# Rows of q dealt to chosen DMA engines: one batch or three

## The chip, the core and the metric

The kernel runs on one core of a Trainium2 chip. The metric is device time in microseconds (us), the median of several runs. A core has five engines with their own instruction streams: PE (matrix products and transposes), DVE and ACT (elementwise work, PSUM to SBUF copies, activations), POOL (here little but the issue of loads) and SP (the issue of the first load and of the outputs). Sixteen DMA engines move data between HBM and SBUF for all of them. A transfer that POOL issues is laid out over DMA engines row by row, each engine works through its own queue in order, and a transfer has landed when all sixteen engines have given their completion mark.

## The reference

Inputs are q, k and v, each (8 batches, 8 heads, 576 rows, 64), the weights `moe_w_r` and `moe_w_i`, each (64 modes, 512, 512), and `moe_w_ch` (512, 512), all float32. Cut to what matters:

```python
scores = scale * np.matmul(q, k.transpose(0, 1, 3, 2))
mask = (rel >= 0) & (rel < 64)                 # causal, a window of 64
attn = softmax(np.where(mask, scores, -1e9))
x = matmul(attn, v) -> (batch, 576, 512)       # heads side by side

X = np.fft.rfft(x, axis=1)                     # along the 576 rows
Yr = Xr @ w_r[m] - Xi @ w_i[m]                 # for each of the first 64 modes m
Yi = Xr @ w_i[m] + Xi @ w_r[m]
y = np.fft.irfft(Y, n=S, axis=1)
u = x + y
return u + np.maximum(u @ w_ch, 0.0)
```

127 weight matrices of 1 MB are read once (mode 0 has no imaginary part), besides 28 MB of q, k, v. The output is 9.4 MB.

## The kernel before

**Attention (0 to about 142 us).** For each batch, `load` brings q, k and v as raw rows in bf16 (the DMA casts): tile `rq` holds `[128, 2, 18 * 64]`. Partition p of half x holds 18 consecutive sequence rows of one head: four heads make the lower half, four the upper one. `transpose_units` gives twelve units for a batch; `part` turns six of the 18 rows' blocks at a time on PE against an identity matrix (`ident_bf`) and copies the result to `qT`, `kT` or `vT`, `vback` turns v once more. `scores`, `weigh` and `mask` make windows of scores, exponentials on ACT and the weighted sums; `dft` and `dft_turn` make the 64 modes of x into `XQ`. PE's and POOL's orders are written out by hand in this part; DVE's and ACT's are the scheduler's. A unit that has read a raw tile calls `refill`, which issues the load of the same tensor two batches on (two buffers each), and with it one weight.

**Modes (about 142 to 392 us).** `half(i)` takes weight i through sixteen products of 128 x 16 against `XQ`; `issue` refills the ring of weight buffers as they are read. In between, PE works on the product with `w_ch` and on the inverse transform. **Tail.** `final` adds, rectifies and stores through SP.

All loads but the first k are issued by POOL, in the order of the program. Eight completion semaphores are used in turn, so a transfer's issue waits for the landing of the transfer eight before it. In a transfer of 128 rows, each DMA engine takes eight rows.

**One q is dealt out unevenly.** `UNEVEN` is batch 7's q. Its lower half is issued as 125 rows for five DMA engines (25 each), the upper half as a plain transfer of 128 rows, then the three rows left over and a small transfer of 22 rows of 16 elements into `aside`. The view `"(r a) c -> a r c"` puts five outermost, and row r * 5 + a goes to partition a * 25 + r, so the rows stand in another order on the partitions. `part` undoes that: for the lower half of this q it uses `back` in place of `ident_bf`, a matrix that DVE makes from `ident_bf` with two copies (L262, L263). Transfers over fewer than sixteen engines begin, as the code has it, where the one before ended, in turn; the small transfer over eleven engines brings the turn round to its beginning.

In issue order the POOL transfers are counted from 0; the q of batches 5, 6 and 7 are 24, 30 and 36 (to 39).

Of the kernel before, what the change touches and what calls it, by code (L numbers as in the profile page):

```python
# [11 lines left out]
BF16 = mybir.dt.bfloat16  # L12
# [8 lines left out]
def view(ap, off, dims):  # L21

    return bass.AP(ap.tensor, ap.offset + off, [list(ap.ap[0])] + [list(d) for d in dims])
# [3 lines left out]
def kernel(  # L27
# [10 lines left out]
    nc = tc.nc  # L38
    B, H, S, D = q.shape
# [8 lines left out]
    RUN = S // 32  # L48
# [6 lines left out]
    def evac(o, i, on_act):  # L55

        if on_act:
            return nc.scalar.copy(out=o, in_=i)  # L58
        return nc.vector.tensor_copy(out=o, in_=i)  # L59
# [10 lines left out]
    ident_bf = consts.tile([128, 128], BF16, name="ident_bf")  # L70
# [19 lines left out]
    acons = p1.enter_context(tc.tile_pool(name="acons", bufs=1, side="right"))  # L90
# [12 lines left out]
    def raw_tile(which):  # L103
        return rawp.tile([128, 2, RUN * D], BF16, name="r" + which)

    def runs(b, which):
        return RAW[which][b].rearrange("(x g) (p c) d -> (g p) x (c d)", g=4, c=RUN)

    UNEVEN = (B - 1, "q")
    FEW, MORE = 5, 25
    LOT = FEW * MORE
    aside = acons.tile([2 * (16 - FEW), 16], BF16, name="aside")
    back = acons.tile([128, 128], BF16, name="back")

    def load(b, which):
        r = raw_tile(which)
        if (b, which) == UNEVEN:
            lower, upper = [RAW[which][b, x * H // 2:(x + 1) * H // 2].rearrange("g (p c) d -> (g p) (c d)", c=RUN)  # L120
                            for x in range(2)]
            nc.gpsimd.dma_start(out=r[:LOT, 0, :], in_=lower[:LOT].rearrange("(r a) c -> a r c", a=FEW))
            nc.gpsimd.dma_start(out=r[:, 1, :], in_=upper)
            nc.gpsimd.dma_start(out=r[LOT:, 0, :], in_=lower[LOT:])
            nc.gpsimd.dma_start(out=aside, in_=lower[:2 * (16 - FEW), 0:16].rearrange("(r a) c -> a r c", a=16 - FEW))
        else:
            nc.gpsimd.dma_start(out=r, in_=runs(b, which))
        raws[b, which] = r
# [65 lines left out]
    with tc.manual_schedule(engines=ALL_FOUR):  # L194
# [3 lines left out]
        with tc.tile_pool(name="tmpf", bufs=1, side="right") as tmp:  # L198
            mo = tmp.tile([128, NM], FP32, name="mo")
            to = tmp.tile([128, NT], FP32, name="to")  # L200
            nc.gpsimd.iota(mo, pattern=[[1, NM]], base=0, channel_multiplier=0,
                           allow_small_or_imprecise_dtypes=True)
            nc.gpsimd.iota(to, pattern=[[128, NT]], base=0, channel_multiplier=1,
                           allow_small_or_imprecise_dtypes=True)
            nc.gpsimd.memset(ident, 0.0)
            nc.gpsimd.affine_select(out=ident, in_=ident, compare_op=ALU.not_equal, fill=1.0,
                                    base=0, pattern=[[-1, 128]], channel_multiplier=1)
            load(0, "q")
            load(0, "v")
            for t0, t1 in ((0, 3), (3, NT)):  # L210
                n = t1 - t0
                mt = tmp.tile([128, 2, n * NM], FP32, name="mtf")
                nc.vector.tensor_tensor(out=view(mt, 0, [[NM, n], [1, NM]]), in0=view(mo, 0, [[0, n], [1, NM]]),
                                        in1=view(to, t0, [[1, n], [0, NM]]), op=ALU.mult)
                gen_trig(tmp, mt, n * NM, trigF[:, t0:t1, 0:NM], trigF[:, t0:t1, NM:2 * NM], "f")
                if t0 == 0:
                    nc.vector.tensor_copy(out=ident_bf, in_=ident)
        nc.scalar.activation(out=spark, in_=ident[:, 0:1], func=ACT_F.Exp)
        raws[0, "k"] = raw_tile("k")
        for c, engine in enumerate((nc.vector, nc.gpsimd, nc.vector)):  # L220
            cc = slice(6 * D * c, 6 * D * (c + 1))
            engine.tensor_copy(out=raws[0, "k"][:, :, cc], in_=k_first[:, :, cc])
        load(1, "k")
        for i in range(4):
            half = i % 2
# [24 lines left out]
    def transpose_units(b):  # L250

        rk, rq, rv = (raws.pop((b, which)) for which in "kqv")
        qT = qtp.tile([128, 4, S], BF16, name="qT")
        vT = vtp.tile([128, 4, S], BF16, name="vT")
        kT, vt = kTs[b % 2], vts[b % 2]
        qTs[b] = qT

        def part(src, dst, c0, on_act, uneven=False):
            def f():
                ps = ps_misc.tile([128, 6, 128], BF16, name="pst", tag="misc")  # L260
                if uneven and c0 == 0:
                    nc.vector.tensor_copy(out=back, in_=ident_bf)  # L262
                    nc.vector.tensor_copy(out=view(back, 0, [[1, FEW], [FEW, MORE]]),  # L263
                                          in_=view(ident_bf, 0, [[MORE, FEW], [1, MORE]]))
                for c in range(6):
                    for hh in range(2):
                        nc.tensor.transpose(out=ps[64 * hh:64 * hh + 64, c, :],  # L267
                                            in_=src[:, hh, (c0 + c) * D:(c0 + c + 1) * D],
                                            identity=back if uneven and hh == 0 else ident_bf)
                evac(view(dst, c0, [[S, 4], [RUN, 32], [1, 6]]),  # L270
                     view(ps, 0, [[32, 4], [1, 32], [128, 6]]), on_act)
            return f

        def vback(u):
            def f():
                ps = ps_misc.tile([128, 6, 128], BF16, name="psv", tag="misc")
                for i in range(6):
                    a, j = divmod(6 * u + i, 9)
                    if j == 4:
                        parts = [(0, 64, 2 * a, 512), (64, 64, 2 * a + 1, 0)]  # L280
                    else:
                        parts = [(0, 128, 2 * a + (j > 4), 128 * j - (j > 4) * S)]
                    for r0, n, g, t0 in parts:
                        nc.tensor.transpose(out=ps[r0:r0 + n, i, :],  # L284
                                            in_=vT[:, g, t0:t0 + n], identity=ident_bf)
                evac(view(vt, 6 * u * VW, [[18 * VW, 2], [VW, 6], [1, D]]),
                     view(ps, 0, [[D, 2], [128, 6], [1, D]]), u != 1)
                if u:
                    hs = slice(u - 1, u + 2, 2)
                    nc.vector.tensor_copy(out=vt[64:128, 1, hs, 1:9], in_=vt[64:128, 0, hs, 0:8])  # L290
                    nc.vector.tensor_copy(out=vt[0:64, 1, hs], in_=vt[0:64, 0, hs])
            return f

        return [part(rk, kT, 0, True), part(rk, kT, 6, False), part(rk, kT, 12, True),
                part(rv, vT, 0, False), part(rv, vT, 6, True), part(rv, vT, 12, False),
                *(part(rq, qT, 6 * i, i != 1, (b, "q") == UNEVEN) for i in range(3)),
                vback(0), vback(1), vback(2)]

    def head_of(n):
# [48 lines left out]
    def closes(w):  # L348

        return min(-(-8 * w // 9) * 9 or 9, 8 * w + 8)  # L350
# [92 lines left out]
    with tc.manual_schedule(engines=ALL_FOUR):  # L443
        first = transpose_units(0)
        for j in (0, 1, 2, 6, 7, 8):
            first[j]()
            refill(0, j)
            if j in (2, 8):
                warm_up(3)
        for half in range(2):  # L450
            pp = slice(64 * half, 64 * half + 64)
            nc.vector.tensor_copy(out=band2[pp], in_=band[pp, half, :])
        mask(0, 1)
        scores(0)
        for j in (3, 4, 5):
            first[j]()
            refill(0, j)
            warm_up(2)
        for vt in vts:
            nc.vector.memset(vt[:, 0, :, :, 64:66], 1.0)  # L460
        for j in (9, 10, 11):
            first[j]()
            refill(0, j)
        nc.vector.memset(pso, 1.0)
        nc.vector.tensor_copy(out=ident_r, in_=ident)
    with tc.manual_schedule(engines={E.PE, E.Pool}):
# [9 lines left out]
        def unit(b, j):  # L476
            if b not in units:
                units[b] = transpose_units(b)
            units[b][j]()
            refill(b, j)  # L480
            turned(b, j)

        for w in range(NWIN + 1):
# [5 lines left out]
            n = len(todo)  # L489
            if 0 < w < NWIN:  # L490
                scores(w)
            if w:
                cut = closes(w - 1)
# [12 lines left out]
            if w in (NWIN - 4, NWIN - 1):  # L506
                i = (B - 2) % 2 if w == NWIN - 4 else (B - 1) % 2
                spare(kTs[i])
                spare(qtp.tile([128, 4, S], BF16, name="qT"))
            if w in (NWIN - 4, NWIN):  # L510
                i = (B - 2) % 2 if w == NWIN - 4 else (B - 1) % 2
# [386 lines left out]
    for k, (f, delta, n, few) in enumerate(items):  # L898
        i = S_I + k * (T_I - 2 - S_I) // len(items)
# [25 lines left out]
    with tc.manual_schedule(engines=ALL_FOUR):  # L925
# [92 lines left out]
        for k in range(6):  # L1018
# [10 lines left out]
                              in_=view(psys[0], 0, [[2 * B, NC], [2, B], [1, 2]]))  # L1029
# [78 lines left out]
```

## Time and profile before

| | us |
|---|---|
| median of 3 runs | 424.34 (424.32 to 424.75) |
| the profiled execution | 424.43 |
| its span, first to last instruction | 422.7 |
| last weight issued, landed | 375.12, 389.20 |
| from there to the end of the span | 33.5 |
| PE busy | 352.8 (83%) |
| DVE, ACT, POOL busy | 189.0, 159.9, 83.7 |
| software DMA queue, packets' time as a share of 16 engines' span | 96.3% |

How to read it: DMA shares add up the time that packets were under way, and packets of one engine overlap a little, so a full engine shows a share over 1. In views by stretches the columns are the busy time of each engine with the number of instructions, then the granted clock of PE, the DMA share and the GB/s written. In a timeline a row is start, length, engine, line, operation, out<-in, and in brackets the idle time before it and what ended it. "DMA to landing" is the time from the issue to the last of the sixteen completion marks. L numbers are lines of the kernel before.

### The profile page before, as it was taken

The page shows a single profiled execution, that of the slowest core. Times are in us where ns is not written, and L with a number is a line of the kernel's source. Part 1 is how long each engine was busy: PE and PEld are TensorE (multiplying, and loading weights), DVE is VectorE, ACT ScalarE, POOL GpSimd, SP SyncE. Part 2 cuts the span into 40 slices and gives each one's busy share as a digit, 9 for nine tenths or more (in the row PEclk, how much of TensorE's full clock was granted, in tenths as well). Part 3 has the DMA queues.
Part 4 walks back from the last instruction along what each step waited for, and adds up shares of the span by engine and source line. Part 5 has one row for each costly group of instructions (what it writes and reads, how often), then busy time and mean ns, then how long its engine had stood idle before and what let it go on. Part 6 is the DMA issues. An engine that isn't in the chain of part 4 may idle for free.

```text
span 422.7 us, 11472 instructions
## 1 busy us (share of the span) xinstructions
PE 352.8 (83%) x5185; PEld 232.3 (55%) x5185; DVE 189.0 (45%) x361; ACT 159.9 (38%) x267; POOL 83.7 (20%) x149
## 2 busy tenths in 40 slices
PE   7899999999998779955758586757699998998994
PEld 3565666656654566744546455545466565554441
DVE  6576766775764100634342251211114344340895
ACT  5566866766765100122102110200023343330863
POOL 6231322232222230412112011210121212300000
PEclk9999999999999655978666656777569999999998
DMA  8999999999999999999999999999999999996598
GB/s 209 212 213 212 214 214 212 212 213 209 214 214 213 214 214 262 213 215 214 215 214 215 213 215 213 216 213 215 213 215 213 215 213 214 213 215 131 205 371 319
DMA packets 30288, 92.55 MB, mean 219 GB/s; under 512 B 2720, under 2 KB 2720, under 8 KB 30240
## 3 DMA queue, kind: packets, MB, share of 16 engines
q0 software_dynamic: 24992, 81.21, 96.3%
q1 hardware_dynamic: 5248, 10.62, 6.8%
q8 instruction: 40, 0.66, 0.6%
q14 instruction: 8, 0.07, 0.0%
HBM read 162.53 MB, written 9.44 MB: 407 GB/s over the span
## 4 chain that ended last, share of the span: by engine, by line
DMA 45%; PE 39%; DVE 7%; issue 2%; ACT 2%; DVEq 0%; POOLq 0%; ACTq 0%
DMA wms<-in_moe_w_i_dram 23%; DMA wms<-in_moe_w_r_dram 22%; PE psy L638 6%; PE pso L363 6%; PE pst L267 5%; PE psv L284 3%; PE psx L385 3%; PE pss L983 3%; DVE x_sb L371 2%; PE pss L976 2%; PE pss L320 2%; PE pss L339 2%; PE psz L779 2%; DVE vT L59 2%; PE psy L923 2%
## 5 line engine op out<-in xcount | busy, mean ns | idle before, releaser
L779 PE MATMUL psz<-wch,xT 128*128 128x512 f32 x144 | 61.2, 564 | 0.0
L773 DVE CAST xT<-pxt 128x1024 fp32r<-128x1024 bf16 x18 | 22.0, 1224 | 80.7 <-PE pxt L768 80.7
L782 ACT CAST Z<-psz 128x1024 fp32r<-128x1024 f32 x18 | 18.2, 1012 | 100.5 <-PE psz L779 100.5
L345 ACT ACTIVATE et<-pss 128x512 bf16<-128x512 f32 x72 | 39.2, 599 | 13.7 <-PE pss L339 13.7
L638 PE MATMUL psy<-XQ,wms 128*128 128x16 bf16 x624 | 25.0, 192 | 20.1 <-DMA wms<-in_moe_w_i_dram 12.3
L638 PE MATMUL psy<-XQ,wls 128*128 128x16 bf16 x560 | 21.9, 192 | 23.2 <-DMA wls<-in_moe_w_r_dram 14.4
L638 PEld LDWEIGHTS <-wms 128*128 128x128 bf16 x624 | 21.3, 102 | 32.3 <-DMA wms<-in_moe_w_i_dram 15.5
L779 PEld LDWEIGHTS psz<-wch,xT 128*128 128x128 f32 x144 | 34.9, 268 | 5.4
L638 PEld LDWEIGHTS <-wls 128*128 128x128 bf16 x560 | 19.6, 105 | 32.6 <-DMA wls<-in_moe_w_r_dram 17.2
L363 PE MATMUL pso<-vt,et 128*64 128x65 bf16 (+1 forms) x576 | 32.3, 203 | 3.5 <-DVE x_sb L371 1.6
L831 DVE TENSOR_TENSOR Z<-pse,Z 128x1024 fp32r<-128x1024 f32 x16 | 19.6, 1225 | 29.6 <-PE pse L820 29.6
L363 PEld LDWEIGHTS <-et 128*64 128x64 bf16 (+1 forms) x576 | 22.2, 108 | 14.2 <-issue 6.7
L371 DVE TENSOR_TENSOR x_sb<-pso,rcp 128x640 bf16<-128x640 f32 x32 | 26.3, 823 | 0.9
L638 PEld LDWEIGHTS <-wt 128*128 128x128 bf16 x560 | 18.4, 105 | 11.1 <-issue 4.2
L638 PE MATMUL psy<-XQ,wt 128*128 128x16 bf16 x560 | 20.5, 192 | 4.4 <-DMA wt<-in_moe_w_i_dram 1.7
L59 DVE COPY vT<-pst 128x768 bf16<-128x768 bf16 x16 | 15.3, 958 | 12.9 <-PE pst L267 11.3
L1001 ACT ACTIVATE pss<-pss 128x512 f32<-128x512 f32 x35 | 18.5, 581 | 4.7 <-PE pss L983 4.0
L59 DVE CAST YT<-psy 128x256 fp32r<-128x256 f32 x6 | 2.5, 423 | 38.6 <-PE psy L638 38.6
L923 PE MATMUL psy<-trigF,ident_bf 128*128 128x512 bf16 x46 | 18.4, 465 | 0.1
L284 PE MATMUL psv<-ident_bf,vT 128*128 128x128 bf16 (+1 forms) x160 | 15.7, 226 | 0.8 <-DVE vT L59 0.6
L320 PE MATMUL pss<-band,ident_bf 64*64 64x512 bf16 x120 | 16.3, 396 | 0.0
L58 ACT COPY vt<-psv 128x768 bf16<-128x768 bf16 x16 | 12.9, 808 | 8.5 <-PE psv L284 8.4
(198 smaller groups left out, 615.0 us busy)
## 6 DMA issues: line engine op xcount, KB each, us to landing
wt<-in_moe_w_i_dram POOLq DMA_DIRECT2D x19, 512.0 KB, 17.9
wt<-in_moe_w_r_dram POOLq DMA_DIRECT2D x16, 512.0 KB, 17.1
wls<-in_moe_w_r_dram POOLq DMA_DIRECT2D x8, 1024.0 KB, 21.7
wms<-in_moe_w_i_dram POOLq DMA_DIRECT2D x7, 1024.0 KB, 22.0
wms<-in_moe_w_r_dram POOLq DMA_DIRECT2D x7, 1024.0 KB, 21.2
wls<-in_moe_w_i_dram POOLq DMA_DIRECT2D x6, 1024.0 KB, 20.7
rv<-in_v_dram POOLq DMA_DIRECT2D x8, 576.0 KB, 13.0
rq<-in_q_dram POOLq DMA_DIRECT2D x7, 576.0 KB, 14.9
```

The costliest lines, as they stand in the source:

```text
L59: return nc.vector.tensor_copy(out=o, in_=i)
L267: nc.tensor.transpose(out=ps[64 * hh:64 * hh + 64, c, :], in_=src[:, hh, (c0 + c) * D:(c0 + c + 1) * D], identity=back if uneven and hh == ...
L284: nc.tensor.transpose(out=ps[r0:r0 + n, i, :], in_=vT[:, g, t0:t0 + n], identity=ident_bf)
L320: nc.tensor.matmul(out=pss[(2 * w + hh) % 3][64 * half:64 * half + 64, :], lhsT=ident_bf[pp, pp], rhs=view(band[pp], 128 * half, [[0, WIN ...
L345: nc.scalar.activation(out=et[:, hh, :], in_=pss[(2 * w + hh) % 3], func=ACT_F.Exp, scale=EX_SCALE)
L363: nc.tensor.matmul(out=pso[po, hh, block(b, i // 2) * VW:block(b, i // 2) * VW + D + 1], lhsT=et[pk, hh, col:col + 64], rhs=vt[pk, 1 - f % ...
L371: nc.vector.tensor_tensor(out=view(x_sb, b * NT * DM + g * D, [[4 * D, 2], [DM, NT], [1, D]]), in0=view(pso, 0, [[512, 2], [VW, NT], [1, D]]),
L638: nc.tensor.matmul(out=view(psy, off + 2 * B * e, [[1, 2 * B]]), lhsT=w[:, c, 128 * e:128 * e + 128], rhs=XQ[:, m // HM, c, :, 1 - im:3 - ...
L773: nc.vector.tensor_copy(out=o, in_=i)
L779: nc.tensor.matmul(out=psz[s][:, j, :], lhsT=xts[s % 2][0][:, j, 128 * c:128 * c + 128], rhs=wch[:, c, :], start=(c == 0), stop=(c == NC - 1))
L831: nc.vector.tensor_tensor(out=z, in0=ps, in1=z, op=ALU.add)
L923: nc.tensor.matmul(out=o, lhsT=ident_bf, rhs=view(trigF, 0, [[1, DM]]), start=True, stop=True)
```

## The change

Three q are dealt out unevenly in place of one. For each, `UNEVEN` gives the engines n, the rows m for each, the columns c (of 18) that are dealt, and the engines that a small transfer behind steps the turn on:

- batch 5: five engines, 25 rows each; a step of two
- batch 6: two engines, 28 rows each; a step of four
- batch 7: 34 rows in one lot for one engine (written as 17 x 2, which no number up to 16 divides), 16 of the 18 columns; a step of two

The rows left over (3, 72 and 94) follow the upper half in a transfer of their own; for batch 7 the last two columns of all 128 lower rows are a transfer too (128 pieces of 128 elements). The small transfers read k. 5 + 2 + 2 + 4 + 1 + 2 is 16. The three q take thirteen transfers in place of six (4, 4 and 5, where it was 1, 1 and 4). `back` is now one matrix for each of the three forms, and `part` uses it for the lower half of the dealt columns. PE has the same instructions in the same order but for the identity matrix; DVE has four copies more, at the start, right behind the two that it had; POOL has seven transfers more.

```diff
-    UNEVEN = (B - 1, "q")
-    FEW, MORE = 5, 25
-    LOT = FEW * MORE
-    aside = acons.tile([2 * (16 - FEW), 16], BF16, name="aside")
-    back = acons.tile([128, 128], BF16, name="back")
+    UNEVEN = {(5, "q"): (5, 25, RUN, 2), (6, "q"): (2, 28, RUN, 4), (7, "q"): (17, 2, 16, 2)}
+    for lot in UNEVEN.values():
+        assert lot[0] <= 16 or all(lot[0] % d for d in range(2, 17))
+    assert sum((n if n <= 16 else 1) + x for n, m, c, x in UNEVEN.values()) % 16 == 0
+    aside = [acons.tile([34, 16], BF16, name=f"aside{i}") for i in range(len(UNEVEN))]
+    forms = {lot[:2]: acons.tile([128, 128], BF16, name=f"back{lot[0]}") for lot in UNEVEN.values()}
+    made = set()
+
+    def back(key):
+
+        n, m = form = UNEVEN[key][:2]
+        if form not in made:
+            made.add(form)
+            nc.vector.tensor_copy(out=forms[form], in_=ident_bf)
+            nc.vector.tensor_copy(out=view(forms[form], 0, [[1, n], [n, m]]),
+                                  in_=view(ident_bf, 0, [[m, n], [1, m]]))
+        return forms[form]
+
+    def step_on(key, n):
+
+        n, src = (n if n > 1 else 17), k[0, :H // 2].rearrange("g (p c) d -> (g p) (c d)", c=RUN)
+        nc.gpsimd.dma_start(out=aside[list(UNEVEN).index(key)][:2 * n],
+                            in_=src[:2 * n, 0:16].rearrange("(r a) c -> a r c", a=n))
 
     def load(b, which):
         r = raw_tile(which)
-        if (b, which) == UNEVEN:
+        if (b, which) in UNEVEN:
...
-            nc.gpsimd.dma_start(out=r[:LOT, 0, :], in_=lower[:LOT].rearrange("(r a) c -> a r c", a=FEW))
+            n, m, c, behind = UNEVEN[b, which]
+            cut = lower[:n * m].rearrange("(r a) c -> a r c", a=n)
+            nc.gpsimd.dma_start(out=r[:n * m, 0, :c * D], in_=cut[:, :, :c * D])
             nc.gpsimd.dma_start(out=r[:, 1, :], in_=upper)
-            nc.gpsimd.dma_start(out=r[LOT:, 0, :], in_=lower[LOT:])
-            nc.gpsimd.dma_start(out=aside, in_=lower[:2 * (16 - FEW), 0:16].rearrange("(r a) c -> a r c", a=16 - FEW))
+            if c < RUN:
+                nc.gpsimd.dma_start(out=r[:, 0, c * D:], in_=lower[:, c * D:])
+            nc.gpsimd.dma_start(out=r[n * m:, 0, :c * D], in_=lower[n * m:, :c * D])
+            if behind:
+                step_on((b, which), behind)
...
-                                            identity=back if uneven and hh == 0 else ident_bf)
+                                            identity=back((b, which)) if hh == 0 and c0 + c < turned else ident_bf)
```

## The prediction

> **What bounds the kernel now.** I read the page's slices first, then its queues and chain, then the end of the chain, and last what POOL issues around the q of batch 7.
>
> ```profile
> DMA  8999999999999999999999999999999999996598
> GB/s 209 212 213 212 214 214 212 212 213 209 214 214 213 214 214 262 213 215 214 215 214 215 213 215 213 216 213 215 213 215 213 215 213 214 213 215 131 205 371 319
> ...
> q0 software_dynamic: 24992, 81.21, 96.3%
> ...
> q8 instruction: 40, 0.66, 0.6%
> ```
>
> The DMA engines are full and at one rate (213 GB/s written) from the first slice to the 36th; in the attention part and in the tail:
>
> ```profile
> 74.00:110.00 36.00, 35.08 (x753) 23.38 (x749) 24.65 (x46) 25.84 (x46) 10.08 (x17) 1.00 1.09 212
> 110.00:142.00 32.00, 27.71 (x487) 15.88 (x483) 16.80 (x34) 17.22 (x33) 6.36 (x12) 0.97 1.06 214
> ...
> 389.20:422.70 33.50, 27.41 (x137) 13.47 (x137) 24.46 (x40) 19.65 (x37) 0.00 (x0) 0.96 0.76 282
> ```
>
> (Busy PE, weight loads, DVE, ACT, POOL in us, then granted clock, DMA share, GB/s.) The 40 packets of q8 fetch instructions, 16 KB each. The end of the chain of waits:
>
> ```profile
> 374.20 0.90 issue
> 375.10 0.02 POOLq L1103
> 375.12 14.08 DMA wms<-in_moe_w_i_dram
> 389.20 0.05 issue
> 389.25 0.65 PE psy L638 x16
> ```
>
> The last weight is issued 14 us before it lands, and lies behind other rows all that time. What follows it (422.7 - 389.2 = 33.5 us) hangs on its landing alone. So the time is the slowest DMA engine's stream plus a fixed tail, and a change counts by what it does to that engine.
>
> The trace holds sixteen completion marks for each transfer, one an engine. Those of the last transfer, in us against the last of them:
>
> ```
> -6.25 -5.94 -5.36 | -1.90 -1.75 -1.34 -1.21 -0.91 -0.75 -0.57 -0.56 -0.55 -0.48 -0.44 -0.29 0
> ```
>
> Three engines end 5.4 to 6.3 us early; thirteen lie within 1.9 us. The mean is 1.77 us ahead of the last, so a perfect division at no cost would bring 1.77 us. The reason shows in the marks too: after each q8 fetch one engine's marks jump back by 1.0 to 1.4 us and recover part; the fetches' lengths repeat with period eight (893, 893, 949, 944, 936 to 940, 975, 975, 962 ns), so eight engines seem to fetch and eight not. The five that took the 125 rows of batch 7 were among the early ones before and the five last ones right after (0 to 0.65 us behind, the next 2.3 us ahead of them). The three left over are the early three.
>
> **What the old form cost** is seen at the issues on POOL:
>
> ```profile
> 88.97 0.70 POOL L122 DMA_DIRECT2D rq<-in_q_dram  x1 [2.24 <-PE pst L267]
> 89.68 0.57 POOL L123 DMA_DIRECT2D rq<-in_q_dram  x1
> 91.42 0.73 POOL L124 DMA_DIRECT2D rq<-in_q_dram  x1 [1.17 <-DMA rq<-in_q_dram]
> 93.89 0.56 POOL L125 DMA_DIRECT2D aside<-in_q_dram  x1 [1.73 <-DMA wt<-in_moe_w_r_dram]
> ```
>
> In the packet records a 2304-byte row (one q row) starts every 173 ns on an engine, a 4096-byte one every 305. A line through both gives 154 ns for a 2048-byte row and 22 ns for a 256-byte piece (estimates from these rows). The eleven engines outside the five each show 25 four-byte packets 6 ns apart for the 125-row transfer: padding, 0.155 us with its completion. The 3-row transfer and the aside cost an engine outside them some 0.033 us each. Over 35 to 43 (transfers by issue order) the front engine needed 11.42 us where rows and completions alone make 11.20: the padding is paid.
>
> **The change, part by part.** I number engines from the turn's start: 0 to 4 the five lots, then 5, 6 skipped, 7 and 8 the two, 9 to 12 skipped, 13 the one, 14 and 15 skipped. The trace does not number them.
>
> *Rows.* Lower halves of q5, q6, q7. An engine of 0-6 or 9-12 gave 16 even rows (2.77 us) for two of these batches, and the 25-row lot is the same before and after. Now it gives 5 of the 72 rows, 6 of the 94 short rows and 8 pieces: 0.865 + 0.924 + 0.176 = 1.965. That is -0.80 us for eleven engines. 7 and 8: -0.80 + 28 x 0.173 = +4.04. 13: -0.80 + 34 x 0.154 = +4.43. If the remainders are laid out in equal shares from engine 0 (72 as fourteen fives and a two, 94 as fifteen sixes and a four), 14 gets -1.32 and 15 -1.98.
>
> *Padding and small transfers.* Three lots for one, so 28 and 34 more padding packets: 28 x 5.85 ns + 0.01 = 0.175 and 0.21. Two more asides 0.066, three more completions 0.045. Sum +0.50 on an engine outside, +0.32 on 7 and 8, +0.29 on 13. Bounds: 0.11 (seven completions of 0.015, padding hidden) to 1.3 (seven times the 0.18 between an empty transfer's marks and those before it, which would make the eleven 0.5 us later). I take 0.50, since the 11.42 against 11.20 is just what the same prices give for the old form's three.
>
> *Sum by engine:* eleven -0.31; 7 and 8 +4.36; 13 +4.72; 14 -0.82; 15 -1.48. The three early ones end at worst at -5.36 + 4.72 = -0.64 against the old last, so they are not the end. The last one sets the gain: 0.31 if it is one of the eleven; 0.29 + 0.31 = 0.60 if it is 14 or 15, since then the one at -0.29 is last. The engine that is last now is the one that jumped at the fetch at 380.4, so a fetching one, and two of the eight fetching ones are 14 and 15. I take 0.40.
>
> A row bears on the remainders: the three 2304-byte packets of the 3-row transfer are on three of the five lot engines, not on the next in turn, so a remainder starts at the first engine and moves no turn. The Trainium skill, "DMA: Bandwidth & Descriptors", section "Why a DMA increments its semaphore by 16 and not by 1", says that a transfer takes the largest number up to 16 that divides both outermost sizes, from a moving cursor, with an exception for some direct copies that take shares rounded up on all sixteen. By its first rule 94 rows go to two engines; the row above speaks for its exception.
>
> *DVE.* Four more copies at the start:
>
> ```profile
> L262 DVE COPY back<-ident_bf x1: 195/195/195, 3.3 to 3.3; 128x128 bf16<-128x128 bf16 x1
> L263 DVE COPY back<-ident_bf x1: 508/508/508, 3.5 to 3.5; 128x125 bf16<-128x125 bf16 x1
> ```
>
> 2 x 0.195 and two strided ones of 56 and 34 elements, between 0.1 and 0.508 each (0.25 and 0.2 by size): 0.84 us, at most 1.4. They stand ahead of trigF's second half. DVE then sits idle 1.05 us for k's first load (L222), which hides them; ACT's table load and first kT copy (0.50 idle before) come up to 0.35 later, 0.9 at most, and PE with them. POOL's later issues wait for PE's reads, but rows are issued 8 to 18 us before they land, so the stream does not see it: nothing. If that cover were gone it would cost that 0.35.
>
> *POOL and the window.* Seven more issues of 0.53 to 0.73 us, 4 to 5 us, where POOL is busy 10.1 of 36 us (74 to 110). Each transfer waits for the one eight before it, and four or five slots now hold one q, so less is queued. Behind the waiting issue stand k, v of batch 7 and weights. Reckoned forward with the marks of before as due times, the engines keep about 1.5 us in hand; nothing. *PE* has the same transposes, 52 instead of 18 with another identity tile at the same 219 ns. q5 and q6 landed 11 and 13 us ahead of their first transpose, q7 8.9 (108.3 against 117.1); a whole single-engine lot is 5.2 us. Nothing.
>
> The profiled execution took 424.43 (span 422.7 and 1.7 around it), the runs' median is 424.34, so 424.34 - 0.40 = 423.9.
>
> **Rivals.** *The padding is hidden.* If the four-byte packets ride along with rows in flight, eleven engines keep -0.66 to -0.80, and if the last one is 14 or 15 too, the end moves by 0.95 to 1.1: 423.2 to 423.4. For it: marks of an empty transfer come 0.17 to 0.2 us late and part is made good by the next rows. Against: the 0.22 us above.
>
> *The rows hit engines that are not early* (slower). The marks show that three engines are early, not that they stand at 7, 8 and 13; should the 72-row remainder go to a few engines in turn and move it, or engine 7 be a late one, 28 to 34 rows fall on an engine at -1.9 to 0: 4.4 to 4.7 more, less its lead, gives 426.8 to 429; and 94 short rows on two engines would be 47 x 0.154 = 7.2 us in place of 0.92, up to 430. It decides from a lead under 4.4. Against: the five were hit as meant, and the 3 rows moved nothing. The Trainium skill, same page, section "Latency and other measured facts", holds that engines 7 and 15 are usually slower than the others; that would be this case for 7, and no row here tells which engine is which.
>
> *The window runs dry* (slower). With 94-row, 72-row, piece and aside transfers filling slots while a lot of 5.2 us is outstanding, weights are issued later than the front engines need them. The tightest lead in the profile is 353.37 to data at about 356. Losing 1 to 1.5 us on engines at -0.3 ends at 425.0 to 425.6; it decides from 0.3 us lost on any late engine. Against: 1.5 us in hand.
>
> *The single-engine lot is spread after all.* Then 13 stays early, every engine gets 2 rows of 0.154 more and 0.2 less padding: 424.1.
>
> **How the numbers follow.** A difference under 0.2% (0.85 us) is about what a measurement of this kernel can't tell from none. Forecast 0.45 and the spread lot 0.05, both within it; padding hidden 0.30, faster; wrong engines 0.10 and dry window 0.10, slower. Range 423.1 to 425.3: it takes in the first rival and most of the last, and leaves out the wrong engines.
>
> **What would show it.** Marks of the last transfer: the early three within 2 us of the last, the rest unmoved among themselves. Right: the last weight lands 0.3 to 0.6 us sooner (388.6 to 388.9) and the 33.5 us after it stay. Wrong engines: one to three marks 2.5 us or more behind all others. Dry window: a slice between 74 and 130 us with DMA share below the 1.06 to 1.09 of now. Padding hidden: less than 0.1 us between empty marks and the rows behind. If the early three stay at -5, the lots did not go where I put them.

## The result

The change made the kernel slower: 429.09 us (428.80 to 429.51) against 424.34, a ratio of 1.0109 with a 95% interval of 1.0094 to 1.0124: 1.1%, small but clear of the noise. The profiled execution took 428.85, its span is 427.1.

The end of the chain of waits of the changed kernel (start, length, what):

```profile
378.86 0.90 issue
379.76 0.02 POOLq L1125
379.78 13.81 DMA wms<-in_moe_w_i_dram
393.59 0.05 issue
393.64 0.65 PE psy L660 x16
```

The chain is the same, 4.39 us later: the last weight lands at 393.59 and not at 389.20, and 33.5 us follow as before. The whole loss lies ahead of that landing. By stretches, first a line of the kernel before, then the changed kernel:

```profile
176.00:389.20 213.20, 164.60 (x1880) 112.73 (x1879) 68.66 (x133) 47.24 (x68) 35.12 (x58) 0.79 1.05 212
```

```profile
74.00:110.00 36.00, 34.96 (x740) 22.93 (x738) 25.71 (x47) 25.93 (x46) 11.56 (x21) 1.00 1.10 210
110.00:142.00 32.00, 27.09 (x474) 15.57 (x478) 16.11 (x32) 16.29 (x32) 7.81 (x15) 0.94 1.06 214
...
176.00:389.20 213.20, 165.95 (x1873) 115.12 (x1881) 68.87 (x132) 46.84 (x67) 35.01 (x58) 0.76 1.05 212
389.20:393.60 4.40, 3.51 (x32) 1.86 (x28) 0.39 (x1) 0.35 (x1) 0.00 (x0) 1.00 0.06 12
393.50:427.10 33.60, 27.34 (x136) 13.52 (x137) 24.47 (x40) 19.65 (x37) 0.00 (x0) 0.92 0.76 282
```

The attention part, where the edited transfers are, runs at 210 and 214 GB/s (212 and 214 before), and the weights up to 389.20 us at the same 1.05 and 212 GB/s. So the engines taken together did as much in the same time. The loss is what follows: 4.4 us with a DMA share of 0.06, about one engine of sixteen. The sixteen marks of the last transfer say why:

```
before  -6.25 -5.94 -5.36 | -1.90 -1.75 -1.34 -1.21 -0.91 -0.75 -0.57 -0.56 -0.55 -0.48 -0.44 -0.29 0   (0 = 389.20)
after   -6.13 -5.99 -5.97 -5.96 -5.87 -5.84 -5.74 -5.60 -5.59 -5.58 -5.52 -5.36 -5.28 -4.88 -4.85 | 0   (0 = 393.59)
```

One engine alone is 4.85 us behind all others, which have nothing left to load. It fell behind at one transfer. The marks of the last even load ahead of batch 7's lot, and of the lot itself (34 rows for one engine):

```
41  -5.76 -3.99 -3.62 -3.18 -2.96 -2.94 -2.85 -2.68 -2.52 | -1.04 -0.77 -0.50 -0.40 -0.29 -0.28 0   (0 = 105.22)
42  -8.17 -6.48 -6.12 -5.67 -5.45 -5.41 -5.34 -5.14 | -3.49 -3.25 -2.94 -2.78 -2.74 -2.72 -2.48 | 0   (0 = 107.90)
```

The front engine (99.47 to 99.73) took only the padding. The 5.2 us fell on an engine of the middle group, which went from about 102.6 to 107.90. So the lot missed the early engine. (A mark carries no engine's number; from here on the last mark is at least 2.48 us behind the next, so it is one engine's.)

The 28-row lots of batch 6 did go to early engines: at that transfer two of the three front marks (84.73 to 84.90) move to the group that is last, which grows from five marks to seven. Which early engine was missed can be read off too. Over the 72-row transfer the front engine's mark moved by 0.17 us (86.54 to 86.71), as over an empty one, where one moved by 0.43 and the others by 0.81 to 0.95, five rows. Of batch 7's 94 rows it took 0.70 where others took about 1.0. In equal shares from the first engine, the sixteenth gets none of 72 and four of 94. And the small transfer behind batch 7, which steps over the fifteenth and the sixteenth, has two of its 32-byte packets at 101.64 us, where only the front engine then was. The early three are 7, 8 and 15; the change aimed at 7, 8 and 13.

### The profile page after: what moved, and what is told of

It is laid out like the page before. It is cut to its first block, busy times and chain, and to the rows that moved or that the text cites. A ratio compares the mean times of both kernels' runs of the same rounds, so it can differ in the third digit from the quotient of the medians.

```text
span 427.1 us, 11455 instructions
## 1 busy us (share of the span) xinstructions
PE 353.1 (83%) x5156; PEld 233.9 (55%) x5185; DVE 190.0 (44%) x365; ACT 159.7 (37%) x267; POOL 87.6 (21%) x156
## 4 chain that ended last, share of the span: by engine, by line
DMA 47%; PE 35%; DVE 7%; issue 5%; ACT 2%; POOL 0%; DVEq 0%; POOLq 0%; ACTq 0%
DMA wms<-in_moe_w_r_dram 26%; DMA wms<-in_moe_w_i_dram 21%; PE pso L385 6%; PE pst L289 5%; PE psy L660 4%; PE psv L306 3%; PE psx L407 3%; PE pss L1005 2%; DVE x_sb L393 2%; PE pss L998 2%; PE pss L342 2%; PE pss L361 2%; DVE vT L59 2%; ACT vt L58 1%; DVE x_sb L1028 1%
## 5 line engine op out<-in xcount | busy, mean ns | idle before, releaser
L801 PE MATMUL psz<-wch,xT 128*128 128x512 f32 x144 | 63.4, 582 | 0.2 <-DMA wch<-in_moe_w_ch_dram 0.2
L801 PEld LDWEIGHTS psz<-wch,xT 128*128 128x128 f32 x144 | 36.2, 278 | 6.0 <-issue 0.3
L790 PE MATMUL pxt<-ident_bf,x_sb 128*128 128x128 bf16 x144 | 16.8, 291 | 0.0
```

The source lines that it names most:

```text
L801: nc.tensor.matmul(out=psz[s][:, j, :], lhsT=xts[s % 2][0][:, j, 128 * c:128 * c + 128], rhs=wch[:, c, :], start=(c == 0), stop=(c == NC - 1))
```

## The experiments

Theory A is that the lot missed: engine 13 fetches instructions and had no time to spare, and engine 15 is the early one. Rival B: the many transfers starve the queues. Rival C: a lot on one engine is slow wherever it lies. In the experiments, the kernel before measured 424.42.

**The lot on the sixteenth engine.**

```diff
-    UNEVEN = {(5, "q"): (5, 25, RUN, 2), (6, "q"): (2, 28, RUN, 4), (7, "q"): (17, 2, 16, 2)}
+    UNEVEN = {(5, "q"): (5, 25, RUN, 2), (6, "q"): (2, 28, RUN, 6), (7, "q"): (17, 2, 16, 0)}
```

> The 34-row lot of batch 7 moved from the fourteenth to the sixteenth engine of the turn: the small transfer behind batch 6 steps six instead of four, and none is needed behind batch 7. Theory A (the lot hit an engine that fetches instructions, the early one is the sixteenth): engine 13 loses 5.0 us, engine 15 gains them out of a lead of 10 us; the last weight lands at about 388.7 to 388.9 us where the next-to-last engine now stands, time 423.8 to 424.2. Rival B (thirteen transfers for six starve the queues): nothing but one small transfer is gone, so 428.5 to 429. Rival C (34 rows on one engine go slower than 154 ns each, whichever engine it is): above 425.

Measured: 424.00 us, ratio to before 0.9986 (0.9969 to 1.0003). The chain's end and the marks of the last transfer:

```profile
375.13 13.73 DMA wms<-in_moe_w_i_dram
388.86 0.05 issue
388.91 0.65 PE psy L660 x16
```

```
-2.22 -1.98 -1.92 -1.76 -1.68 -1.39 -1.27 -1.13 -0.94 -0.80 -0.78 -0.70 -0.68 -0.49 -0.13 0   (0 = 388.86)
```

The same rows on another engine: 5.1 us less than the change, all sixteen marks within 2.2 us, and the landing 0.34 ahead of before. The only other differences are one small transfer fewer and another over six engines in place of four. C falls, and B nearly: one transfer of the thirteen is gone (the half dose below has all of them). Against the kernel before, the interval holds 1, so this run shows no gain.

**The lot on the fifteenth.** `(6, "q")` with a step of 5, `(7, "q")` with a step of 1.

> The same lot on the fifteenth engine of the turn (steps of five, then one; the step of one is itself 34 small rows on one engine). Theory A: the fifteenth fetches too, so the lot makes it last. It has three rows fewer of the 72 than the fourteenth (0.52 us), and the padding of the extra small transfer costs 0.2: 428.3 to 429. If the early engine were the fifteenth and not the sixteenth, about 424. Rival B: 428.5 to 429 as well.

Measured: 428.53 (four runs, 427.56 to 432.25), ratio 1.0103 (1.0047 to 1.0160).

```profile
379.83 13.82 DMA wms<-in_moe_w_i_dram
393.65 0.05 issue
393.70 0.65 PE psy L660 x16
```

One engine is again last, by 4.43 us, and the early one still led by 10.28 at 351.8 us. Neither 13 nor 14 has time to spare; 15 has.

**Half the dose.** `(7, "q"): (17, 2, 8, 2)`, still on 13.

> The lot stays on engine 13 with 8 of the 18 columns in place of 16: 34 rows of 1024 bytes, about 2.7 us in place of 5.2, and the pieces of the other ten columns go to all engines evenly (0.15 more each). Theory A: the last engine is earlier by 2.4 us, time 426.5 to 426.9. Rival B: the same thirteen transfers, so 428.5 to 429.

Measured: 426.83, ratio 1.0051 (1.0032 to 1.0070).

```profile
377.98 13.82 DMA wms<-in_moe_w_i_dram
391.80 0.05 issue
391.85 0.65 PE psy L660 x16
```

The gap to the next engine shrank from 4.85 to 2.91 us and the time by 2.3, with as many transfers. The loss goes with the bytes on engine 13, and B falls with that.

**Without batch 7's lot.**

```diff
+    UNEVEN = {(5, "q"): (5, 25, RUN, 2), (6, "q"): (2, 28, RUN, 7)}
```

> Only batches 5 and 6 are dealt out (five and two engines), batch 7's q is a plain load. Theory A with padding paid: an engine outside the lots gets 1.38 us of even rows in place of 1.10 of short rows and pieces, 0.21 of padding and 0.1 of extra transfers, so the lot of batch 7 sheds nothing for them: 423.8 to 424.2, no different from the lot on the sixteenth engine. With padding hidden: that one is faster than this by 0.25 us. Rival B: two of three groups of small transfers are left, so about 427.

Measured: 424.14, ratio 0.9994 (0.9972 to 1.0017); the last weight lands at 388.73, and one engine alone is early, by 5.44 us where the next is at 1.95. So the third lot, rightly aimed, gives nothing that can be told (424.00 with it, 424.14 without). That fits padding that is paid, but 0.25 us, the difference if it is hidden, lies within the intervals too; the next run decides that.

**The price of padding by itself.** The kernel before, with this ahead of batch 7's q sixteen times, once for each engine:

```diff
+            nc.gpsimd.dma_start(out=blanks.pop(), in_=src[:34, 0:16].rearrange("(r a) c -> a r c", a=17))
```

> The kernel before with sixteen small transfers more, each 34 rows of 16 elements for one engine, one on each engine of the turn, all ahead of batch 7's q. The data are 17 KB. Padding paid at 5.9 ns a packet: fifteen times 34 packets and its own on every engine, 16 x 0.21 = 3.4 us, 427.6 to 427.9. Padding hidden: sixteen completions of 0.015 to 0.03, 424.6 to 424.9. Rival B (small transfers take slots, the queue runs dry): over 428, with engines idle in the attention part.

Measured: 427.50, ratio 1.0071 (1.0057 to 1.0085), so 3.1 us for 17 KB, 0.19 a transfer. The page's queue line, and a stretch of the attention part, of the kernel before and of this run:

```profile
q0 software_dynamic: 33952, 81.26, 97.0%
```

```profile
20.00:74.00 54.00, 51.46 (x1087) 33.57 (x1082) 37.22 (x67) 36.73 (x64) 13.84 (x22) 1.00 1.09 213
```

```profile
20.00:74.00 54.00, 51.39 (x1076) 33.53 (x1073) 37.95 (x68) 36.68 (x65) 24.62 (x32) 1.00 1.12 205
```

There are 8960 packets more than before's 24992: 16 transfers x 16 engines x 35. Every engine gets as many packets as the one with the rows, and a completion. The DMA share is up (1.12 for 1.09) while the rate falls (205 GB/s for 213): the engines are busy with padding, not idle.

**Laid out anew for 0 to 4, 7, 8 and 15.**

```diff
+    UNEVEN = {(5, "q"): (6, 21, RUN, 2), (6, "q"): (2, 32, RUN, 6), (7, "q"): (6, 9, RUN, 0)}
+            if b == 5:
+                step_on(3, 15)
```

> The lots laid out for the early engines as they now stand (0 to 4, 7, 8, 15), and fewer of them: batch 5 in 126 rows for six engines (15 and 0 to 4, 21 each), batch 6 in 64 rows for 7 and 8 (32 each), batch 7 in 54 rows for 15 and 0 to 4 (9 each); steps of fifteen, two and six between. Against the kernel before, an engine that fetches gives up 2.99 us and takes 0.20 (batch 5, padding and small ones) + 0.94 (four rows, 32 packets of padding) + 0.96 (five rows, 9 of padding): about -0.9 us. Engines 0 to 4 stay as they were, out of a lead of 0.9 us; 7 and 8 take 4.3 more, 15 about 3.3 more. Theory A: 423.3 to 423.7, ahead of the lot on the sixteenth engine (424.0). If division among engines is no longer what sets the end, 424.0.

Measured: 424.00, ratio 0.9990 (0.9981 to 0.9999). And with 12 in place of 9:

> The same with 12 rows each in batch 7 (72 rows for six engines, four left for each of fourteen others): the fetching engines are at -1.1 us, but 0 to 4 at +0.3, so they become the last. Theory A: 423.5 to 424.0, no better than with 9 rows. If padding were hidden, 0.4 us faster than these figures, both.

Measured: 424.22, ratio 0.9997 (0.9988 to 1.0006). Both missed the ranges of Theory A. With 9 rows the kernel is faster than before, by 0.4 us and not by 0.7 to 1.1, and no faster than with the lot on the sixteenth engine (424.00 too). With 12 it is no better than with 9, as expected, but 0.2 us above its 423.5 to 424.0. The marks of the last transfer with 9 rows:

```
-1.89 -1.40 -1.08 -1.05 -1.03 -0.93 -0.90 -0.86 -0.56 -0.55 -0.49 -0.38 -0.37 -0.33 -0.32 0   (0 = 388.65)
```

They are as even as in any kernel here, so little is left to divide. But their mean, 0.76 ahead of the last, is at 387.89, where it was at 387.43 before: evening out has not made the engines done sooner on average. That the added transfers and padding took the 0.46 us is not shown, since the run with 12 rows, which has more padding, has its mean at 387.51. The last one has been last since batch 7's lot (107 us), so it is one that takes lots; I had given 0 to 4 a lead of 0.9 us that at least one engine with lots did not have.

## Why the prediction was wrong

The step that failed is the numbering. That three engines end 5.4 to 6.3 us early was read from marks; that they stand at 7, 8 and 13 was read from where the change aims, which is no row of the profile. All that was summed on it (13 at -5.36 + 4.72 = -0.64, so "they are not the end") fell with it. Engine 13 was a late one, by what the fetches show below the very last, and from 0 with 4.72 more it had to land the last weight 4.72 us later. The landing came 4.39 later, the median 4.75. The prediction's eight fetching engines were wrong in the same way: it counted 15 among them and took 13 out.

Point by point:

- *The bound*: right. The tail after the last landing stayed (33.5 us), and slower meant a slower DMA engine.
- *Rows and padding by engine*: near, as far as marks without numbers show it. The next-to-last mark after the change is at 388.74 (393.59 - 4.85) against 389.20 for the last one before: -0.46, where the sum for engines that get no lot said -0.31. Right behind the last changed transfer the seven marks of the middle group stand at 105.01 on the mean, where eight stood at 105.71: -0.7, where the sums (six at -0.31, one at -0.82) make -0.4. The price of padding, 0.21 for 34 packets, measured 0.19.
- *The gain of 0.3 to 0.6, had the aim been right*: with the lot on engine 15 the last weight landed 0.34 earlier and the time was 424.00 where 423.9 was forecast. That agrees, but the run's interval holds no gain as well, so the size is not shown.
- *The remainders*: right. They come in rounded-up shares from the first engine and move no turn: the skipped engines of the small transfer behind batch 7 were found where the turn should put them. The Trainium skill ("DMA: Bandwidth & Descriptors", section "Why a DMA increments its semaphore by 16 and not by 1") has an exception by which some direct copies go out in shares rounded up over sixteen engines. The trace agrees: the front engine's 0.17 us over the 72 rows is a share of none.
- *The rival "rows hit engines that are not early"*: this is what happened, just above its 426.8 to 429 and with the sign that was named for it (one mark over 2.5 us behind all others), though by neither way that I named. The turn was where it should be and engine 7 was early. The Trainium skill, same page, section "Latency and other measured facts", has engines 7 and 15 as usually slower. If its numbers are those of the turn, this case differs: 7, 8 and 15 are the early ones, by over 5 us. The chance of 0.10 was too low for an assumption with no row behind it.
- *Padding hidden, dry window, lot spread*: none of them is the cause. The first falls with the 8960 packets and their 3.1 us, the third with the one mark that moved 5.2 us. The window did run dry, but only for the front engine: from the small transfer behind batch 7's q it took 11.50 us over the next four loads (102.14 to 113.64) where it was 9.52 before (103.59 to 113.11). It had that time to spare; the late engines show no such gap.
- *DVE*: hidden, as said. The six copies took this:

```profile
L126 DVE COPY back<-ident_bf x3: 186/186/194, 3.3 to 3.5; 128x128 bf16<-128x128 bf16 x3
L127 DVE COPY back<-ident_bf x3: 293/368/504, 3.6 to 4.0; 128x125 bf16<-128x125 bf16 x1, 128x56 bf16<-128x56 bf16 x1, 128x34 bf16<-128x34 bf16 x1
```

They overlap, so the next DVE step came 0.24 us later (4.05 for 3.81), and ACT's table load 0.27 (5.79 for 5.52), inside the cover.

Why 13 and 14 are late, and 15 is not, the kept traces show, since after the change the last and the front mark are each one known engine's. The last marks, engine 13's, come about 2.45 us apart for loads of 512 KB and 4.9 for loads of 1 MB, but three times 1.1 to 1.3 us later than that: 3.53 us to the mark at 121.47, 6.17 to 181.7 and 6.07 to 305.2. Each time a fetch began just ahead (117.5, 179.5, 302.8), and these are the 17th, 25th and 33rd of forty. With the lot on the fifteenth engine the last mark jumps like this behind the fetches at 147.1, 224.3 and 343.6, again every eighth. The front marks after the change, engine 15's, show no such step from 113.64 to 346.66 us. So 13 and 14 fetch and 15 does not, and forty fetches over eight engines, five each at about 1.1 us, are about the lead of 5.4 to 6.3 us that the early three had (an estimate from these steps).

The lengths of the fetches come in the same order in every run, with few exceptions, so they tell engines apart: 14's take 961 or 962 ns, and 13's are the 974 or 975 right ahead of them. In the kernel before, the fetch at 380.4 has 13's place in that order, and the engine that jumped there was the last one. So by this order (an inference: no row numbers an engine) the 34 rows went to the very engine that the end waited for. No run took the fetches away.

## What to carry to other kernels

When work is dealt to particular DMA engines, a transfer ends with its slowest engine, so a lot on the wrong one costs nearly its whole length (5.2 us of rows, 4.75 of time), and one on the right one brought nothing here that the runs tell from none (424.00 with it, 424.14 without). Which engine is early must be read from a row that names it: a transfer whose shares differ by engine (none, two or five rows of 72) does that. And a transfer for few engines is not free for the others: count its rows on one engine as packets on all sixteen.

## What the runs showed that I had not expected

A transfer for one engine gives all the others as many four-byte packets as that one has rows, about 5.5 ns each (0.19 us for 34), and they are paid in full. That leaves little to gain: dealt over sixteen engines, 34 rows of 0.154 us would be 0.33 us on each (an estimate from these rows), and the padding takes 0.19 of that.

A late engine also holds back the early ones: a transfer is issued when the one eight before it has landed on all engines. After the change the front engine led the last by 10.06 us until 356.7, and by 7.17 at 359.1; its mark took 5.28 us over a load that took the others about 2.5, so its queue had run out. At the end the lead is 6.13. That cost nothing here, since it was not the last, but it hides in the final marks how much an engine could have taken.
